# Reading a quad's query and key rows by chunk of tokens, and storing its maxima's rows in two transfers

## The chip, the cores and the metric

The kernel runs on one core of a Trainium2 chip. Five engines work side by side, each from its own list of instructions, in that list's order: TensorE (PE in the profile, its weight loads PEld), VectorE (DVE), ScalarE (ACT), GpSimd (POOL) and SyncE (SP). They wait for each other by semaphores. Transfers between device memory and the core's SBUF are issued here by SP and by ACT; each of the two has a DMA queue of its own, q1 (SP) and q10 (ACT), and 16 DMA engines serve both. The metric is the device time of one execution in microseconds, lower is better.

## The reference, cut to what matters

One transformer block with modulated layer norms: attention over a sliding window of 256 tokens with 32 heads of 20 channels, then an MLP, on 2048 tokens of 640 channels, in float32.

```python
def _A_ref(x, wqkv, wo):
    H = 32; Dh = D // H; W = 256
    qkv = (x @ wqkv).reshape(B, S, 3, H, Dh).transpose(2, 0, 3, 1, 4)
    q, k, v = qkv[0], qkv[1], qkv[2]
    scores = jnp.einsum("bhqd,bhkd->bhqk", q, k) * (Dh ** -0.5)
    mask = (idx[:, None] - idx[None, :] >= 0) & (idx[:, None] - idx[None, :] < W)
    scores = jnp.where(mask[None, None], scores, -1e9)
    p = _softmax(scores, axis=-1)
    o = jnp.einsum("bhqk,bhkd->bhqd", p, v)
    return o.transpose(0, 2, 1, 3).reshape(B, S, D) @ wo
...
h = _layernorm(x) * (1 + ca) + sa
x = x + ga * _A_ref(h, A_wqkv, A_wo)
h = _layernorm(x) * (1 + cb) + sb
x = x + gb * _B_ref(h, B_w1, B_b1, B_w2, B_b2)
```

## The kernel before

**Stages.** Up to some 50 us the kernel computes the modulation, the first layer norm and the first projections. From there (the first score product starts at 49.6 us) to about 690 us runs the attention, with the rest of the projections and then the output projection laid into it, piece by piece. From 690 us on the MLP runs; the change touches nothing of it.

**How the attention is tiled.** The 2048 tokens are two halves (`HALF` = 1024) of eight query blocks of 128 tokens (`NQB`), the 32 heads are eight quads of four (`QUADS`). The main loop (L1263) has one iteration for each half, quad and query block, `t` = 0 to 127, and some more to drain. So a quad takes eight iterations. In iteration `t` the program does two things for two different quads.

- *Scores for the maximum* (`s_batch`, `s_max`): one query block against its three key blocks, on PE into the tile `s`; DVE masks and reduces them to a maximum for each query and head, `nm`. This is quad `t // 8`.
- *Scores for the softmax* (`e_batch`, `e_mask`, `e_exp`), `LAG` = 11 iterations later: the same products, but transposed, into `e`, with the maximum already subtracted; ACT takes the exponential into `pt`, DVE and POOL mask, and PE then multiplies with the values (tile `o`).

The subtraction costs nothing extra on PE. Queries and keys of a quad lie in SBUF as `qbuf` and `kbuf`, two heads' pairs to a tile, each head on 60 partitions (20 channels, three parts each that make up float32 products). Two further partitions of each head, rows 60 and 61, hold the negative maximum as a high and a low part in `qbuf` and ones in `kbuf`. The `s` products read 60 rows, the `e` products 62. So the first `e` matmul of a quad has to wait until the quad's maxima stand in rows 60 and 61 of `qbuf`.

**How the maxima get there.** After the quad's last query block DVE splits `nm` into the two parts (`m_split`, tile `mh`). In the next iteration, `t` a multiple of 8, PE transposes `mh` into the PSUM tile `pm`, and ACT copies it to the SBUF tile `mt` (`m_rows`). Then ACT issues four DMAs from `mt` into rows 60 and 61 (`m_store`): two, for the first pair of heads, at the end of this iteration, and two, for the second pair, at the end of the next one. Each moves 16 rows of 512 B, 8 KB. The quad's first `e` product stands in the third iteration after that multiple of 8.

**How queries and keys get there.** The projections' results are written to device memory (`q_scr`, `k_scr`) by SP, when a unit of 128 channels and 512 tokens (`CHUNK`) is done (`rows_out`), and read back by SP in the layout above (`rows_in`). `rows_in` is called once for the queries and once for the keys of each quad and half, and issues two DMAs, one for each head of a pair: 60 partitions by two pairs by 1024 tokens, 480 KB, and in the second half 1280 tokens of keys, 600 KB. The slots for this, `qb_` and `kb_`, are four deep (`NSLOT`).

**What sets the order.** `plan` maps iteration and quarter to pieces of work. For the reads (L1182) a quad's `due` is its first iteration; its queries are read at `due - READ`, 8 iterations ahead, its keys one iteration later, both in the last quarter, but not before two iterations after the last projection that they need (`over_at`), and not before their slot is free. So a quad's reads usually fall in the first two iterations of the quad before it, the same in which ACT stores that quad's predecessor's maxima.

**DMA semaphores.** The framework gives every DMA, of SP and ACT alike, one of eight semaphores in turn, and a DMA isn't issued before the transfer that had its semaphore last, eight DMAs back, has landed. An engine that waits for this holds everything behind it in its list.

All engine calls go through one helper, so every row of the profile names L112, and instructions are told apart by their tiles.

Of the kernel before, what the change touches and what calls it, by code (L numbers as in the profile page):

```python
# [21 lines left out]
HALF = 1024  # L22
HEADS = (0, 2, 1, 3)
NQB = HALF // P
QUADS = H // 4
CHUNK = 512
VW = 21
VQ = 4 * VW + 11
NSLOT = 4
NVB = 5  # L30
LAG = 11
# [15 lines left out]
    (1, "q00", "k00", "q10", "k10", "q01", "k01", "q11", "k11", "v0", "v1", "q2", "k2", "q3", "k3", "v2", "v3", "q4", "k4", "v4"),  # L47
)
FAST = 10
READ = 8  # L50
LAST = 112

V_COST = 1.7
# [38 lines left out]
def f32(ap):  # L92
    return ap.bitcast(F32)
# [24 lines left out]
def block_kernel(ctx: ExitStack, tc: tile.TileContext, x, wqkv, wo, w1, b1, w2, b2, c, crow, wmod, wcol, sel, outT):  # L118
    core = tc.nc
    nc = Ordered(tc)  # L120
# [256 lines left out]
    qb_ = [att.tile([P, 2, HALF], F32R, name=f"qbuf{i}") for i in range(NSLOT)]  # L377
    kb_ = [att.tile([P, 2, 256 + HALF], F32R, name=f"kbuf{i}") for i in range(NSLOT)]
# [11 lines left out]
    def qbuf(half, pair):  # L390
        return qb_[(half * QUADS + pair // 2) % NSLOT][:, pair % 2]

    def kbuf(half, pair):
        return kb_[(half * QUADS + pair // 2) % NSLOT][:, pair % 2]

    def rows_in(half, quad, kind):

        i = (half * QUADS + quad) % NSLOT
        src = qk_scr[kind].rearrange("(Q a e d) l s -> Q e (d l) a s", a=2, e=2, d=DH)[quad]
        to = qb_[i] if kind == 0 else kb_[i] if half else kb_[i][:, :, 256:]  # L400
        c0 = half * (HALF - 256 * kind)
        for e in range(2):
            nc.sync.dma_start(f32(to[64 * e : 64 * e + 60]), src[e][:, :, c0 : c0 + to.shape[2]])
        if kind:
            there.add((half, quad))

    def vblk(half, quad, kb):
        if half == 1 and kb < 0:
# [1 line left out]
        return vq_[(half * QUADS + quad) % NVB][:, kb]  # L410

    writes, first = [], {}
    there = {(0, 0)}
    quads = {}
    now = [-1]
    done_v = set()
# [103 lines left out]
    def score_banks(kind, name):  # L520
        t = pools[kind].tile([P, 4 * 384], F32, tag=kind, name=name)
        return t, t.rearrange("p (h n) -> p h n", n=384)
# [45 lines left out]
    def s_batch(it):  # L568
        half, quad, qb, g = it["key"]
        if qb == 0:  # L570
            it["quad"]["nm"] = att.tile([P, 4, NQB], F32, tag="nm", bufs=2, name=f"nm{half}_{quad}")
        t, s = score_banks("s", f"s{half}_{quad}_{qb}")
        c0 = 384 - P * min(g + 1, 3)
        parts = []
        for h in HEADS:
            pair, r = 2 * quad + h // 2, slice(64 * (h % 2), 64 * (h % 2) + 60)
            assert (half, quad) in there
            k0 = 256 + (qb - 2) * P + c0
            parts.append([(
                c0, 384 - c0, qbuf(half, pair)[r, qb * P : (qb + 1) * P],  # L580
                lambda off, n, k=kbuf(half, pair), r=r, k0=k0: k[r, k0 + off : k0 + off + n],
            )])
        return (t, parts), s, c0
# [5 lines left out]
        nc.vector.tensor_reduce(it["quad"]["nm"][:, :, it["key"][2]], s[:, :, max(c0, P) : 384], AX.X, ALU.max)  # L589

    mh = att.tile([P, P], F32R, name="mh")
    mh_parts = mh[:, 0:64].rearrange("p (h l q) -> p h l q", h=4, l=2)
    nc.vector.memset(f32(mh)[:, 64:P], 0.0)

    def m_split(it):
        nm, hi, lo = it["quad"]["nm"], mh_parts[:, :, 0], mh_parts[:, :, 1]
        nc.vector.tensor_scalar(hi, nm, -1.0, None, ALU.mult)
        nc.vector.scalar_tensor_tensor(lo, nm, -1.0, f32(hi), ALU.mult, ALU.subtract)

    def m_rows(it):  # L600
        half, quad, _, _ = it["key"]
        ps = aside([P, P], f"pm{half}_{quad}")
        transpose(ps, f32(mh), idn)
        mt = att.tile([64, P], F32, tag="mt", name=f"mt{half}_{quad}")
        nc.scalar.copy(mt, ps[0:64])
        it["mt"] = mt

    def m_store(it, a):
        half, quad, _, _ = it["key"]
        for e in range(2):  # L610
            r = 64 * e + 60
            i = HEADS.index(2 * a + e)
            nc.scalar.dma_start(f32(qbuf(half, 2 * quad + a)[r : r + 2, :]), it["mt"][16 * i : 16 * i + 16])


    def e_parts(it):
# [9 lines left out]
    def e_batch(it):  # L626
        half, quad, i = it["key"]
        t, e = score_banks("e", f"e{half}_{quad}_{i}")
        parts = []
        for h in HEADS:  # L630
            pair, r = 2 * quad + h // 2, slice(64 * (h % 2), 64 * (h % 2) + 62)
            parts.append([(
                col, n, kbuf(half, pair)[r, 256 + kb * P : 256 + (kb + 1) * P],
                lambda off, n, q=qbuf(half, pair), r=r, q0=q0: q[r, q0 * P + off : q0 * P + off + n],
            ) for kb, q0, q1, col, n in e_parts(it)[0]])
        return (t, parts), e

# [460 lines left out]
    def put(t, h, *gos):  # L1098
        plan.setdefault((t, h), []).extend(gos)
# [47 lines left out]
    lo, hi = 4.0, 16.0  # L1147
    for _ in range(30):
        room = (lo + hi) / 2
        lo, hi = (lo, room) if lay_units(room)[0] <= LAST else (room, hi)  # L1150
    _, where, turns = lay_units(hi)
    ready_w = [(seq[0][0], 0)]
    for i, key, c2, pieces, ev in where:
        t0, t1 = pieces[0][0], pieces[-1][0]
# [26 lines left out]
            put(t1, 3, *ev)  # L1181
    for half in range(2):  # L1182
        over_at = {}
        for _, key, _, pieces, _ in where:
            if key[0] == half:
                over_at[key[1:]] = pieces[-1][0]
        for quad in range(QUADS):
            if half or quad:
                js = range(4 * quad * DH // P, (4 * quad * DH + 4 * DH - 1) // P + 1)
                due = 8 * (half * QUADS + quad)  # L1190
                t = due - READ
                for kind in range(2):
                    t = max([t, due - 8 * NSLOT + LAG + 8] + [over_at.get((kind, j), -9) + 2 for j in js])
                    assert t < due - 1, (half, quad, t)
                    put(max(t, 0), 3, lambda half=half, quad=quad, kind=kind: rows_in(half, quad, kind))
                    t += 1
    for n, ((g, at), lo) in enumerate(zip(((2, 0), (4, 1), (3, 2), (5, None)), MODS)):
        steps, rows = mod_steps(g, at)
        spread(plan, [step(1, f) for f in steps], lo[0], lo[1])
        t = int(lo[1])  # L1200
        for f in rows:
            t = take_aside(t, f) + 1
    for ch, when in turns.items():
# [7 lines left out]
        t = when  # L1211
        for kt in range(KT):
            t = take_aside(t, lambda gos=turn[3 * kt : 3 * kt + 3]: [go() for _, go in gos]) + 1
# [34 lines left out]
    s_items, e_items = [], []  # L1248
# [7 lines left out]
    n = len(s_items)  # L1256
# [6 lines left out]
    for t in range(n + LAG + PVLAG + 4):  # L1263
        now[0] = t
        si = s_items[t] if t < n else None
        u = t - LAG
        ei = e_items[u] if 0 <= u < n else None
        if t == n:
            sco_ctx.close()
            pools["t"] = ctx.enter_context(  # L1270
                tc.tile_pool(name="ps_t", bufs=1, space=PSUM, side="left", reuse_waits="tile")
            )
        turn_m = 8 <= t <= n and t % 8 == 0
        batches = []
# [12 lines left out]
        if ei and ei["kbs"]:  # L1287
            e_exp(ei, e)
        if si:
            s_max(si, *got)  # L1290
            if t % NQB == NQB - 1:
                m_split(si)
        rows_out()
        for h in range(4):
            if h == 1 and turn_m:
                m_rows(s_items[t - 1])
            for go in plan.pop((t, h), ()):
                go()
        for a in range(2):
            if 8 <= t - a <= n and (t - a) % 8 == 0:  # L1300
                m_store(s_items[t - a - 1], a)
        for key in pv_at.get(t, ()):
            pv_store(*key)
    assert not writes and not plan
# [19 lines left out]
    for ch in range(nch):  # L1324
        yhi, ylo = ([y[:, kt] for kt in range(KT)] for y in yT[ch % 2])
        ts = slice(ch * CHUNK, (ch + 1) * CHUNK)
        lo, hi = (4, 9) if ch == 0 else (4 * ch + 5, 4 * ch + 9)
# [98 lines left out]
```

## Time and profile before

| | before |
|---|---|
| median of 3 runs | 1093.26 us (1092.42 to 1093.41) |
| the profiled execution's own time | 1094.34 us |
| its span, from the first to the last instruction | 1092.3 us |
| granted TensorE clock, mean over the span | 0.941 |
| attention from the first quad's maxima on, 97.0 to 690.3 us | 593.3 us, PE busy for 505.88 |
| MLP, 690 to 1092.3 us | 402.3 us, PE busy for 397.69 |
| DMA traffic | 91392 packets, 152.88 MB, 140 GB/s over the span |

The profile names a group of instructions by engine, operation and tiles, output first: `e<-qbuf,kbuf` is the softmax score product, `qbuf<-mt` a store of maxima, `qbuf<-q_scr` and `kbuf<-k_scr` reads of rows. ACTq and SPq are those engines' lists of issues. A wait is put down to what ended it. Busy time of PE is modelled, and a busy PE need not be PE at its peak. Over 40 equal slices of the span the granted clock (in tenths) and the share of the 16 DMA engines' time go like this:

```profile
PEclk8899899999899999989976968899999999999999
DMA  8357658726548717871573111424442244213313
```

The DMA engines are busy for much of the attention and little of the MLP, and the clock falls below full in some slices of the attention.

### The profile page before, as it was taken

Reading aid. Unit: us, or ns where it says so; the run is one execution under the profiler, and the core shown is the slowest. Engines: PE = TensorE matmul, PEld = TensorE weight load, DVE = VectorE, ACT = ScalarE, POOL = GpSimd, SP = SyncE. Lnnn points to the kernel's source line nnn. Section 1 sums busy time; section 2 is a strip of 40 time slices with the busy share of each in tenths; the row PEclk is TensorE's granted clock in tenths of the full one; section 3 lists DMA queues with packets and bytes.
Section 4 is the critical chain, followed back from the end, with each engine's and each line's share of the span. In section 5 each row is a group of like instructions: output and inputs, shape, how many; then the busy total and the mean of one; then the engine's idle time right before and its main releaser. Section 6 shows DMA issues by size and latency. Waiting matters only on the chain.

```text
span 1092.3 us, 19853 instructions
## 1 busy us (share of the span) xinstructions
PE 986.5 (90%) x7712; PEld 776.2 (71%) x7712; DVE 579.0 (53%) x943; ACT 444.2 (41%) x773; POOL 510.9 (47%) x702
## 2 busy tenths in 40 slices
PE   7998899699798888889987887999999999999998
PEld 6665666566576666667665665788888888888886
DVE  6643767687476586757656854345443334332212
ACT  3633354365454344435443444443343323333222
POOL 4233445466565244634442654366555545642221
PEclk8899899999899999989976968899999999999999
DMA  8357658726548717871573111424442244213313
GB/s 278 134 188 188 196 163 255 198 85 188 167 143 255 204 58 242 254 203 49 157 182 115 54 41 59 133 89 151 150 126 75 83 130 139 61 49 102 104 49 108
DMA packets 91392, 152.88 MB, mean 140 GB/s; under 512 B 8068, under 2 KB 41476, under 8 KB 91300
## 3 DMA queue, kind: packets, MB, share of 16 engines
q1 hardware_dynamic: 80932, 142.71, 43.7%
q10 hardware_dynamic: 10368, 8.92, 2.7%
q8 instruction: 61, 1.00, 0.4%
q14 instruction: 31, 0.25, 0.1%
HBM read 99.17 MB, written 51.58 MB: 138 GB/s over the span
## 4 chain that ended last, share of the span: by engine, by line
PE 63%; DMA 15%; DVE 8%; POOL 5%; ACT 4%; issue 3%; SPq 1%; ACTq 0%; POOLq 0%; DVEq 0%
PE h L112 15%; PE out L112 15%; PE pp L112 10%; DMA qbuf<-mt 6%; PE wo L112 6%; PE o L112 5%; PE e L112 5%; PE s L112 4%; ACT pt L112 3%; DVE nm L112 2%; DVE e L112 2%; DMA kbuf<-k_scr 2%; DMA wraw<-in_wqkv 1%; DVE s L112 1%; POOL wlo L112 1%
## 5 line engine op out<-in xcount | busy, mean ns | idle before, releaser
L112 POOL TENSOR_SCALAR_AFFINE_SELECT pt<-pt 128x512 f32<-128x512 f32 x192 | 129.1, 673 | 205.7 <-ACT pt L112 185.7
L112 PE MATMUL e<-qbuf,kbuf 62*128 62x128 f32 (+2 forms) x792 | 128.2, 342 | 58.2 <-DMA qbuf<-mt 37.0
L112 PEld LDWEIGHTS e<-qbuf,kbuf 62*128 62x128 f32 x792 | 89.3, 205 | 102.3 <-ACT pt L112 43.2
L112 DVE TENSOR_REDUCE nm<-s 128x4 f32<-128x1024 f32 (+1 forms) x128 | 152.6, 1193 | 4.4
L112 POOL TENSOR_TENSOR w2lo<-w2r,w2hi 128x640 fp32r<-128x640 f32 x48 | 75.6, 1574 | 154.3 <-ACT w2hi L112 154.1
L112 ACT ACTIVATE pt<-e 128x1024 f32<-128x1024 f32 (+1 forms) x120 | 133.8, 1115 | 31.6 <-DVE e L112 30.7
L112 ACT COPY oT<-o 128x128 f32<-128x128 f32 x128 | 34.0, 266 | 251.7 <-PE o L112 228.3
L112 PE MATMUL s<-kbuf,qbuf 60*128 60x256 f32 (+2 forms) x744 | 118.9, 315 | 19.3 <-DVE nm L112 12.1
L112 DVE COPY_PREDICATED e<-mask_t,e 128x512 f32<-128x512 uint32 x96 | 66.6, 694 | 123.2 <-PE s L112 66.8
L112 PE MATMUL pp<-hhi,whi 128*128 128x512 f32 x275 | 122.7, 446 | 3.7 <-ACT hhi L112 1.5
L112 PEld LDWEIGHTS s<-kbuf,qbuf 60*128 60x128 f32 x744 | 99.0, 200 | 36.4 <-issue 10.3
L112 PE MATMUL pp<-hlo,whi 128*128 128x512 f32 x275 | 115.4, 420 | 2.7 <-POOL hlo L112 2.7
L112 PE MATMUL pp<-hhi,wlo 128*128 128x512 f32 x275 | 115.7, 421 | 1.0 <-POOL wlo L112 1.0
L112 DVE CAST ghi<-g 128x512 fp32r<-128x512 f32 x48 | 25.2, 525 | 171.2 <-ACT g L112 171.1
L112 PE MATMUL o<-pt,vbuf 128*32 128x128 f32 x2688 | 111.8, 301 | 0.4 <-ACT oT L112 0.4
L112 POOL TENSOR_TENSOR wlo<-wraw,whi 128x128 fp32r<-128x128 f32 x185 | 81.2, 470 | 39.7 <-ACT whi L112 39.7
L112 PE MATMUL h<-yhi,w1hi 128*128 128x512 f32 x240 | 95.8, 399 | 0.4 <-ACT oT L112 0.4
L112 PE MATMUL out<-ghi,w2hi 128*128 128x512 f32 x240 | 96.2, 401 | 0.0
L112 PE MATMUL h<-ylo,w1hi 128*128 128x512 f32 x240 | 94.0, 392 | 0.0
L112 PE MATMUL h<-yhi,w1lo 128*128 128x512 f32 x240 | 93.9, 391 | 0.0
L112 PE MATMUL out<-ghi,w2lo 128*128 128x512 f32 x240 | 93.9, 391 | 0.0
L112 PE MATMUL out<-glo,w2hi 128*128 128x512 f32 x240 | 93.9, 391 | 0.0
(166 smaller groups left out, 1846.9 us busy)
## 6 DMA issues: line engine op xcount, KB each, us to landing
w2r<-in_w SPq DMA_DIRECT2D x48, 320.0 KB
qbuf<-q_scr SPq DMA_DIRECT2D x30, 480.0 KB
wraw<-in_wqkv SPq DMA_DIRECT2D x38, 320.0 KB
q_scr<-stage SPq DMA_DIRECT2D x20, 512.0 KB
k_scr<-stage SPq DMA_DIRECT2D x20, 512.0 KB
kbuf<-k_scr SPq DMA_DIRECT2D x16, 600.0 KB
o_scr<-oT ACTq DMA_DIRECT2D x64, 128.0 KB
kbuf<-k_scr SPq DMA_DIRECT2D x14, 480.0 KB
```

The source lines that it names most:

```text
L112: return self.tc.keep_in_program_order(op(*args, **kw))
```

## The change

It has three parts.

- `rows_in` takes a chunk `c2` as well and reads 512 tokens of queries or keys (the first chunk of keys in the second half reads 768, with the 256 tokens of the half before). A quad's four DMAs become eight of 240 KB (360 KB for those keys).
- The planner asks for each chunk by its own need: chunk 0 is due with the quad's first iteration, chunk 1 four iterations later; `READ` is 7. A chunk waits only for the projections of its own 512 tokens.
- The rows of `mh` are put in another order (head of the pair, part, pair, block), so that one DMA can fill both pairs of one head's rows. `m_rows` issues the two DMAs, 32 rows of 512 B each, right behind the copy to `mt`; `m_store` and its calls are gone.

```diff
-READ = 8
+READ = 7
...
-    def rows_in(half, quad, kind):
+    def rows_in(half, quad, kind, c2):
...
-        to = qb_[i] if kind == 0 else kb_[i] if half else kb_[i][:, :, 256:]
-        c0 = half * (HALF - 256 * kind)
+        to = (qb_, kb_)[kind][i]
+
+        c0, n = c2 * CHUNK, CHUNK
+        if kind and (c2 or not half):
+            c0 += 256
+        elif kind:
+            n += 256
+        t0 = half * HALF + c0 - 256 * kind
         for e in range(2):
-            nc.sync.dma_start(f32(to[64 * e : 64 * e + 60]), src[e][:, :, c0 : c0 + to.shape[2]])
+            nc.sync.dma_start(f32(to[64 * e : 64 * e + 60, :, c0 : c0 + n]), src[e][:, :, t0 : t0 + n])
...
-    mh_parts = mh[:, 0:64].rearrange("p (h l q) -> p h l q", h=4, l=2)
+    mh_parts = mh[:, 0:64].rearrange("p (e l r) -> p e l r", e=2, l=2)
...
-        nm, hi, lo = it["quad"]["nm"], mh_parts[:, :, 0], mh_parts[:, :, 1]
+        nm, hi, lo = it["quad"]["nm"].rearrange("p (e a) q -> p e (a q)", e=2), mh_parts[:, :, 0], mh_parts[:, :, 1]
...
         nc.scalar.copy(mt, ps[0:64])
-        it["mt"] = mt
-
-    def m_store(it, a):
-        half, quad, _, _ = it["key"]
         for e in range(2):
-            r = 64 * e + 60
-            i = HEADS.index(2 * a + e)
-            nc.scalar.dma_start(f32(qbuf(half, 2 * quad + a)[r : r + 2, :]), it["mt"][16 * i : 16 * i + 16])
+            to = qb_[(half * QUADS + quad) % NSLOT][64 * e + 60 : 64 * e + 62]
+            nc.scalar.dma_start(f32(to), mt[32 * e : 32 * e + 32])
...
-                t = due - READ
-                for kind in range(2):
-                    t = max([t, due - 8 * NSLOT + LAG + 8] + [over_at.get((kind, j), -9) + 2 for j in js])
-                    assert t < due - 1, (half, quad, t)
-                    put(max(t, 0), 3, lambda half=half, quad=quad, kind=kind: rows_in(half, quad, kind))
-                    t += 1
+                for c2 in range(2):
+                    t = due + 4 * c2 - READ
+                    for kind in range(2):
+                        t = max([t, due - 8 * NSLOT + LAG + 8] + [over_at.get((kind, j, c2), -9) + 2 for j in js])
+                        assert t < due + 4 * c2 - 1, (half, quad, c2, t)
+                        put(max(t, 0), 3, lambda half=half, quad=quad, kind=kind, c2=c2: rows_in(half, quad, kind, c2))
+                        t += 1
...
-        for a in range(2):
-            if 8 <= t - a <= n and (t - a) % 8 == 0:
-                m_store(s_items[t - a - 1], a)
```

On ACT, at the fourth quad of the first half (iterations 32 and 33; `oT` and `pt` belong to the quad before it, `stage` and `pf` to a projection, `whi` to its weights), this stood before:

```order
L112 COPY mt_3_2114<-pm_3_2112 64x128
L112 DMA qbuf_96<-mt_3_2114 2x8x128 x2
L112 DMA o_scr<-oT_2_1_2038 128x256
L112 COPY oT_2_2_2166<-o_2_4_2153 128x128
L112 ACTIVATE pt_2_6_2168<-e_2_6_2133 128x1536
L112 CAST whi_2182<-wraw_1952 128x640
L112 ACTIVATE stage_1_4_2190<-pp_1_4_2105 128x512
L112 ACTIVATE pf_1_4_2192<-pp_1_4_2105 128x512
L112 DMA qbuf_96<-mt_3_2114 2x8x128 x2
L112 COPY oT_2_2_2166<-o_2_5_2209 128x128
```

and this stands there now:

```order
L112 COPY mt_3_2124<-pm_3_2122 64x128
L112 DMA qbuf_96<-mt_3_2124 2x16x128 x2
L112 DMA o_scr<-oT_2_1_2048 128x256
L112 COPY oT_2_2_2174<-o_2_4_2161 128x128
L112 ACTIVATE pt_2_6_2176<-e_2_6_2141 128x1536
L112 CAST whi_2190<-wraw_1958 128x640
L112 ACTIVATE stage_1_4_2198<-pp_1_4_2115 128x512
L112 ACTIVATE pf_1_4_2200<-pp_1_4_2115 128x512
L112 COPY oT_2_2_2174<-o_2_5_2215 128x128
```

The second pair's stores are gone from behind `pf`, and the pair behind the copy moves twice the rows. Where a projection's evacuation falls in iteration 32 itself, as at the first quad, the stores also move ahead of its `stage` and `pf`.

On SP, about the same place (`qbuf_94` and `kbuf_98` are the sixth quad's slots, `stage` rows written by a projection, `wraw` weights), before:

```order
L112 DMA wraw_2103<-in_wqkv 128x640
L112 DMA qbuf_94<-q_scr 60x2x1024 x2
L112 DMA kbuf_98<-k_scr 60x2x1024 x2
L112 DMA k_scr<-stage_1_4_2190 128x2x512
L112 DMA k_scr<-stage_1_4_2190 128x512
L112 DMA wraw_2227<-in_wqkv 128x640
L112 DMA wraw_2340<-in_wqkv 128x640
L112 DMA q_scr<-stage_0_4_2458 128x2x512
```

and now:

```order
L112 DMA wraw_2113<-in_wqkv 128x640
L112 DMA qbuf_94<-q_scr 60x2x512 x2
L112 DMA k_scr<-stage_1_4_2198 128x2x512
L112 DMA k_scr<-stage_1_4_2198 128x512
L112 DMA wraw_2233<-in_wqkv 128x640
L112 DMA kbuf_98<-k_scr 60x2x512 x2
L112 DMA wraw_2348<-in_wqkv 128x640
L112 DMA qbuf_94<-q_scr 60x2x512 x2
L112 DMA kbuf_98<-k_scr 60x2x512 x2
L112 DMA q_scr<-stage_0_4_2468 128x2x512
```

Four reads that stood together ahead of a projection's stores are now four pairs with the stores and weights between them. The lists of PE, DVE and POOL keep their order.

More of the change, by code (lines that the diff above doesn't have):

```diff
@@ L394, in kbuf @@
         return kb_[(half * QUADS + pair // 2) % NSLOT][:, pair % 2]
-    def rows_in(half, quad, kind):
+    def rows_in(half, quad, kind, c2):
         i = (half * QUADS + quad) % NSLOT
         src = qk_scr[kind].rearrange("(Q a e d) l s -> Q e (d l) a s", a=2, e=2, d=DH)[quad]
-        to = qb_[i] if kind == 0 else kb_[i] if half else kb_[i][:, :, 256:]
-        c0 = half * (HALF - 256 * kind)
+        to = (qb_, kb_)[kind][i]
[5 more added lines that the diff above has]
+        t0 = half * HALF + c0 - 256 * kind
         for e in range(2):
-            nc.sync.dma_start(f32(to[64 * e : 64 * e + 60]), src[e][:, :, c0 : c0 + to.shape[2]])
-        if kind:
-            there.add((half, quad))
+            nc.sync.dma_start(f32(to[64 * e : 64 * e + 60, :, c0 : c0 + n]), src[e][:, :, t0 : t0 + n])
+        there.add((half, quad, kind, c2))
     def vblk(half, quad, kb):
@@ L412, in block_kernel @@
     writes, first = [], {}
-    there = {(0, 0)}
+    there = {(0, 0, kind, c2) for kind in range(2) for c2 in range(2)}
     quads = {}
@@ L576, in s_batch @@
             pair, r = 2 * quad + h // 2, slice(64 * (h % 2), 64 * (h % 2) + 60)
-            assert (half, quad) in there
+            assert all((half, quad, kind, qb // 4) in there for kind in range(2))
             k0 = 256 + (qb - 2) * P + c0
@@ L1183, in block_kernel @@
         over_at = {}
-        for _, key, _, pieces, _ in where:
+        for _, key, c2, pieces, _ in where:
             if key[0] == half:
-                over_at[key[1:]] = pieces[-1][0]
+                over_at[(*key[1:], c2)] = pieces[-1][0]
         for quad in range(QUADS):
```

## The prediction

> **What bounds the kernel now.** I read the page first, for the engines' shares and the chain that ended last.
>
> ```profile
> span 1092.3 us, 19853 instructions
> ...
> PE 986.5 (90%) x7712; PEld 776.2 (71%) x7712; DVE 579.0 (53%) x943; ACT 444.2 (41%) x773; POOL 510.9 (47%) x702
> ...
> PE h L112 15%; PE out L112 15%; PE pp L112 10%; DMA qbuf<-mt 6%; PE wo L112 6%; PE o L112 5%; PE e L112 5%; PE s L112 4%; ACT pt L112 3%; DVE nm L112 2%; DVE e L112 2%; DMA kbuf<-k_scr 2%; DMA wraw<-in_wqkv 1%; DVE s L112 1%; POOL wlo L112 1%
> ```
>
> PE is busy for 90% of the span, and PE's matmuls lead the chain. Its largest entry that is no arithmetic is the store of the maxima's rows, `qbuf<-mt`, with 6%. So the second view is PE's waits between 60 and 690 us, the attention part (columns: sum in us, times, longest).
>
> ```profile
> PE e L112 <- DMA qbuf<-mt: 37.0, 14, 4.4
> PE e L112 <- ACT pt L112: 20.7, 23, 2.7
> PE s L112 <- DVE nm L112: 12.1, 23, 1.3
> PE s L112 <- DMA kbuf<-k_scr: 6.6, 3, 3.4
> ```
>
> The change touches the first row and the fourth: 37.0 + 6.6 = 43.6 us in which PE stood and a DMA released it. Where they fall is shown by the third view, busy time by stretch. I cut it where `mt` is copied out of PSUM, once per quad, so each row is one quad's period.
>
> ```profile
> core 0: us, PE busy (x) PEld busy (x) DVE busy (x) ACT busy (x) POOL busy (x), PEclk, DMA share, GB/s
> 97.00:135.60 38.60, 31.71 (x226) 22.55 (x224) 22.50 (x28) 15.29 (x28) 17.69 (x27) 0.87 0.65 197
> ...
> 169.00:200.30 31.30, 29.90 (x320) 21.91 (x321) 22.41 (x30) 16.60 (x32) 17.39 (x30) 1.00 0.72 215
> 200.30:239.90 39.60, 31.08 (x326) 22.39 (x326) 27.62 (x43) 18.98 (x34) 22.27 (x36) 0.91 0.49 141
> 239.90:274.80 34.90, 30.91 (x330) 22.35 (x332) 26.52 (x44) 18.68 (x36) 23.16 (x44) 1.00 0.65 181
> 274.80:314.60 39.80, 31.72 (x328) 23.60 (x329) 23.12 (x31) 18.13 (x31) 25.12 (x37) 0.91 0.53 162
> ...
> 349.80:385.80 36.00, 31.68 (x331) 23.24 (x329) 21.19 (x26) 13.95 (x31) 9.36 (x17) 0.95 0.71 188
> 385.80:419.00 33.20, 29.94 (x328) 22.22 (x327) 25.31 (x33) 16.04 (x30) 15.65 (x24) 1.00 0.37 122
> 419.00:454.30 35.30, 31.81 (x364) 23.76 (x362) 27.42 (x37) 16.29 (x28) 18.86 (x26) 1.00 0.78 231
> 454.30:493.90 39.60, 33.33 (x358) 24.83 (x357) 22.77 (x29) 15.66 (x31) 17.64 (x27) 0.91 0.81 221
> 493.90:525.90 32.00, 30.84 (x358) 22.86 (x357) 22.42 (x29) 16.79 (x34) 16.04 (x26) 1.00 0.13 43
> 525.90:566.40 40.50, 33.17 (x354) 24.39 (x352) 24.26 (x30) 17.57 (x32) 17.73 (x23) 0.90 0.65 178
> 566.40:604.80 38.40, 29.81 (x334) 24.10 (x335) 25.39 (x32) 13.21 (x24) 12.78 (x17) 0.67 0.46 126
> ```
>
> The work is nearly the same in each (PE busy for 30 to 33 us), but a period lasts 31.3 to 34.9 us in some and 35.3 to 40.5 in others. One long period in order of time, from the timelines of ACT, SP and PE (start, length, what; the idle time before it in brackets):
>
> ```profile
> 200.06 0.26 ACT L112 COPY mt<-pm 64x128 f32<-64x128 f32 x1 [0.47 <-PE pm L112]
> 200.35 1.28 ACTq L112 DMA_DIRECT2D qbuf<-mt  x2
> ...
> 202.88 1.57 SPq L112 DMA_DIRECT2D qbuf<-q_scr  x2
> ...
> 204.19 0.62 ACTq L112 DMA_DIRECT2D qbuf<-mt  x1
> ...
> 205.28 0.89 SPq L112 DMA_DIRECT2D kbuf<-k_scr  x2
> ...
> 207.55 0.62 ACTq L112 DMA_DIRECT2D qbuf<-mt  x1
> ...
> 212.21 0.38 PE L112 MATMUL e<-qbuf,kbuf 62*128 62x256 f32 x1 [2.85 <-DMA qbuf<-mt]
> 216.41 0.69 PE L112 MATMUL e<-qbuf,kbuf 62*128 62x384 f32 x1 [3.83 <-DMA qbuf<-mt]
> ```
>
> The copy `mt` is done at 200.32. Two of its four stores go out at once, the other two only at 204.19 and 207.55, in the midst of the next quad's row reads. PE has nothing else from 212.21 - 2.85 = 209.36, and loses 2.85 + 3.83 = 6.7 us. The chain shows how long such late stores fly (start, us from issue to landing):
>
> ```profile
> 103.00 8.21 DMA qbuf<-mt
> ...
> 207.55 8.81 DMA qbuf<-mt
> ...
> 280.97 9.51 DMA qbuf<-mt
> ```
>
> That the reads hold them is seen in the DMA queues' packets in two short windows, 135.7 to 141.3 us, just after two stores went out behind a quad's four reads, and 604.8 to 607.2, where two went out with no read about (packets, MB, share of 16 engines; q1 is SP's queue, q10 ACT's):
>
> ```profile
> q1 hardware_dynamic: 425, 1.34, 98.8%
> ...
> q10 hardware_dynamic: 9, 0.01, 0.4%
> ```
>
> ```profile
> q10 hardware_dynamic: 36, 0.02, 2.8%
> ```
>
> In the first, 9 packets of ACT's queue moved in 5.6 us, though two and then three 8 KB stores were out (a store is 16 rows of 512 B). In the second, 36 moved: both stores, within 2.4 us.
>
> **The change part by part.**
>
> *The stores go out earlier.* All of `mt` is now sent right behind the copy. At 620 ns an issue, the second is out by 1.3 us; landing takes 2.4 us more in the quiet case and some 7 in the crowded one. So it lands 2.4 to 8.3 us after the copy, and PE's need came 209.36 - 200.32 = 9.0 us after it. Bounds: all 37.0 us go, or a third of them stays where the queue is full.
>
> *The reads leave the stores' place.* The reads that began in iterations 0 and 1 of a quad's eight now come in iterations 1, 2, 5 and 6, and the stores in 0. The last read starts over one iteration ahead of the store, 4.1 us (the four periods of 31.3 to 34.9 us have a mean of 32.9, in eight iterations); its 480 KB take 2.0 us at the 1.34 MB in 5.6 us of the window above. I take the queue as free in most quads.
>
> *The reads are smaller and some are later.* Bytes stay: a quad's four reads of 480 KB, at 0.24 MB/us, are 8.2 us of a 33 us period. Half-length rows cost between nothing more and, if a packet of 2 KB took as long as one of 4, 8.2 us more of the queue. The nearest row of 2 KB packets, the scratch stores between 345.2 and 347.6 us, is at the first end, so I take nothing:
>
> ```profile
> DMA packets 499, 0.94 MB, mean 390 GB/s; under 512 B 43, under 2 KB 43, under 8 KB 499
> ```
>
> The cover is the time to the need: queries are asked for seven iterations ahead and keys six, 25 to 29 us. One row speaks against this cover, SP's own longest wait; it serves its list in order:
>
> ```profile
> SPq L112 <- POOL stage L112: 174.6, 33, 23.2
> ```
>
> If such a wait falls ahead of a read, the scores wait. But the key reads that the planner put late for want of their producer, three to five iterations ahead, now have a first chunk four to six ahead and a second at six, so I expect the 6.6 us of `PE s <- DMA kbuf<-k_scr` to go.
>
> The Trainium skill speaks against halving: "DMA: Bandwidth & Descriptors", Rules for kernel authors, says to coalesce many small transfers into one, and that under 64 KB one pays mostly overhead. By it the 60 added reads are a loss, and the stores, 8 KB to 16 KB, a gain. The trace doesn't show the loss as a time of the queue: the window with 425 packets is full to 98.8%, so reads follow each other without a hole.
>
> *Issue time.* The split of the maxima on DVE keeps its two instructions of 32 elements. SP has 60 issues more, ACT 32 fewer:
>
> ```profile
> L112 ACTq DMA_DIRECT2D qbuf<-mt x64: 620/621/1240, 97.5 to 648.2; - x64
> L112 SPq DMA_DIRECT2D qbuf<-q_scr x30: 337/386/1634, 71.7 to 562.1; - x30
> L112 ACTq DMA_DIRECT2D o_scr<-oT x64: 321/327/716, 126.7 to 692.1; - x64
> ```
>
> SP: 60 x 0.386 = 23 us over 600, while it mostly waits; nothing. ACT: 32 x 0.62 = 19.8 us less if the larger store costs no more to issue, nothing less if it costs twice (1.24). The store of `oT` has eight times the rows and half the cost, so I take the first. It is ACT time beside a PE that is the bound, with ACT busy for half of each period: nothing in the sum, and if its cover is gone some 1 us a quad.
>
> *What is late next.* Without the stall, PE meets the waits that the short periods have. There, PE idles 31.30 - 29.90 = 1.4, 34.90 - 30.91 = 4.0, 33.20 - 29.94 = 3.3 and 32.00 - 30.84 = 1.2 us, 2.5 on average. In the eight periods of 35.3 us and more it idles 6.9, 8.5, 8.1, 4.3, 3.5, 6.3, 7.3 and 8.6, in all 53.5. If these come down to 2.5 to 3 each, 53.5 - 8 x 2.8 = 31 us go. By PE's waits alone it would be 43.6; by the periods' length (307.8 us for the eight, against 8 x 32.9) 44.6. I take the idle time, the lowest, since waits that end together with another one give back a part: **-31 us**.
>
> The profiled execution took 1094.34 us, 2.0 around its span of 1092.3, and 1.1 more than the median of 1093.26. 1094.3 - 31 = 1063.3 in its terms, 1062 in the median's; I say **1063**.
>
> **The rivals.**
>
> *Half is given back.* PE's next waits, on `pt` (20.7 us) and `nm` (12.1), grow: while PE stood, ACT, DVE and POOL caught up, and POOL is busy for 22 to 25 us of the long periods at 200 and 274. For it: 23 + 23 such waits already. Against it: the short period at 239 has POOL busy for 23.16 us and takes 34.9. It would leave half, -16: 1078 (1071 to 1088).
>
> *Slower: ACT is held by its own issue.* A DMA isn't issued until the transfer that used its semaphore before, eight DMAs back, has landed; the waits tell of this on ACT:
>
> ```profile
> ACT oT L112 <- DMA qbuf<-mt: 6.5, 3, 2.8
> ```
>
> The stores now stand in mid-iteration ahead of a projection's evacuation and the next `pt`. Where the transfer eight back is a row read issued two iterations before and held by SP, ACT stops with all behind it, and PE runs dry. Priced by the wait at 207.55 (204.19 to 207.55 for one issue) at up to 4 us, in all sixteen quads, that is +64 - 31: 1127; in ten, 1103. It decides where that read lands over 5 us after the copy. Against it: the same waits stood ahead of the same `pt` before, at the iteration's end, and the transfers waited for are half as long.
>
> *The stores still wait.* Scratch stores and weights fill the queue as the reads did, the landing stays at 8 to 9 us, and the split reads only stretch over more of it: -4, 1090 (1088 to 1095). Against it: the quiet window's 36 packets.
>
> *More goes than the waits.* The granted clock is 0.87 to 0.91 in five of the eight periods and 1.00 in all four short ones here. If PE's work there is stretched by it, up to 0.13 x 38.6 + 0.09 x (39.6 + 39.8 + 39.6) + 0.10 x 40.5 = 20 us come on top: 1043. Against it: PE's busy time is just 1 to 2 us longer there. "TensorE: Matmul & The Clock Gate" of the Trainium skill (Why this matters for your kernels) asks for no PE-idle gaps over some 3 us, or the clock falls to half; the rows agree with it in sign.
>
> **How the numbers follow.** Forecast (1050 to 1070) 0.60; half given back 0.20; stores still wait 0.06; ACT held 0.09; clock on top 0.05. The range 1050 to 1087 takes in the first two. A change within 0.2%, about what a measurement of this kernel can tell, is 1091.1 to 1095.4: 0.06. Faster 0.85, slower 0.09.
>
> **What would show it.** PE's wait `e <- DMA qbuf<-mt` under 6 us in all and `s <- DMA kbuf<-k_scr` near nothing; the long periods at 33 to 36 us and the short ones as they were; the clock at 0.95 or more up to 566 us; the chain without `qbuf<-mt`. I am wrong if ACT's waits on DMAs grow past 20 us, if PE's waits on `pt` or `s <- DMA` take the room, or if the stores still land 8 us after the copy.

## The result, and the profile after

| | before | after |
|---|---|---|
| median | 1092.84 us (4 runs, 1088.07 to 1093.41) | 1043.09 us (4 runs, 1040.07 to 1045.16) |
| the profiled execution's own time | 1094.34 us | 1042.79 us |
| its span | 1092.3 us | 1040.4 us |
| granted clock, mean | 0.941 | 0.962 |

The ratio is 0.9552, 95% interval [0.9516, 0.9588]: about 50 us faster. The forecast was 1063 with a range of 1050 to 1087. The sign was right and the size was not: 31 us were forecast, and the time lies 7 us below the range.

The page of the changed kernel: span, engines, the granted clock in slices, the chain by engine and by line.

```profile
span 1040.4 us, 19908 instructions
...
PE 972.3 (93%) x7712; PEld 766.4 (74%) x7712; DVE 576.1 (55%) x943; ACT 443.7 (43%) x773; POOL 513.0 (49%) x702
...
PEclk8999999999899999999968978999999999999999
...
PE 75%; DVE 10%; ACT 5%; DMA 3%; POOL 3%; issue 2%; SPq 1%; ACTq 0%; POOLq 0%; DVEq 0%
PE h L112 16%; PE out L112 16%; PE pp L112 14%; PE wo L112 7%; PE o L112 6%; PE e L112 6%; PE s L112 5%; DVE e L112 3%; DVE nm L112 3%; ACT pt L112 3%; DVE s L112 2%; PE ppo L112 2%; DMA kbuf<-k_scr 1%; PE yt L112 1%; PE psx L112 1%
```

The store `qbuf<-mt`, 6% of the chain before, is no entry any more. But PE's own busy time also fell, from 986.5 to 972.3 us with the same 7712 products: a part which the prediction's sum left out. PE's waits between 60 and 690 us begin like this now:

```profile
PE e L112 <- ACT pt L112: 27.7, 28, 2.8
PE s L112 <- DVE nm L112: 9.7, 20, 1.3
```

Both DMA rows, 37.0 and 6.6 us before, are gone. The two that remain were 20.7 and 12.1, so together they grew by 4.6 us: little was given back.

Where the span went is read by cutting both runs at the first copy of `mt` and 402.6 us before the end. The columns are those of the prediction's periods (stretch, length, PE busy, PEld, DVE, ACT, POOL, PEclk, DMA share, GB/s). Before:

```profile
96.80:689.70 592.90, 505.48 (x5350) 376.01 (x5352) 384.61 (x531) 268.03 (x489) 296.28 (x454) 0.91 0.54 156
0.00:96.80 96.80, 82.99 (x413) 64.98 (x414) 52.97 (x138) 40.79 (x70) 33.55 (x57) 0.91 0.61 197
```

After:

```profile
94.40:637.80 543.40, 490.88 (x5360) 364.91 (x5363) 384.66 (x531) 267.95 (x491) 297.33 (x454) 0.94 0.57 172
0.00:94.40 94.40, 83.40 (x413) 66.03 (x414) 50.06 (x138) 40.70 (x69) 34.00 (x57) 0.93 0.57 191
```

The attention is 49.5 us shorter. Length less PE's busy time is its idle time: 592.90 - 505.48 = 87.4 before, 543.40 - 490.88 = 52.5 after, so **34.9 us are idle time and 14.6 us are busy time**. Each figure is from one execution. That PE's products got faster does not hang on that choice: the mean granted clock is 0.961 to 0.967 in the four runs of the changed kernel, and 0.932 to 0.949 in the twelve runs of the kernel before that stood beside the first experiments. But those twelve runs took 1088.03 to 1101.7 us, the longest at the lowest clock, so 14.6 us is a size good to a few us only.

The first 95 us bring 2.4 more. The last 402.6 us hold the same work in both, with PE busy for 398.0 of them.

The same eight quads whose periods were long before, cut at the copies of `mt` again:

```profile
94.70:127.10 32.40, 29.64 (x226) 21.32 (x224) 22.52 (x29) 15.00 (x27) 17.50 (x27) 0.95 0.82 258
...
190.30:223.20 32.90, 31.03 (x326) 21.97 (x324) 27.46 (x43) 19.09 (x34) 22.41 (x36) 0.95 0.55 169
...
257.00:293.40 36.40, 32.48 (x328) 23.79 (x329) 23.91 (x31) 18.20 (x31) 25.32 (x37) 0.91 0.53 165
...
324.00:354.70 30.70, 29.63 (x330) 22.02 (x328) 21.53 (x27) 13.86 (x30) 10.08 (x18) 1.00 0.69 191
...
387.90:421.20 33.30, 31.91 (x364) 23.74 (x362) 27.76 (x37) 16.29 (x28) 18.86 (x26) 1.00 0.82 264
421.20:453.80 32.60, 31.04 (x359) 22.83 (x357) 22.73 (x29) 15.70 (x31) 17.68 (x27) 1.00 0.87 254
...
485.80:517.50 31.70, 29.68 (x354) 22.12 (x352) 23.86 (x30) 17.66 (x31) 17.75 (x23) 1.00 0.67 195
517.50:553.50 36.00, 27.88 (x333) 22.34 (x335) 24.64 (x33) 13.10 (x24) 13.32 (x17) 0.76 0.61 164
```

Their sum is 266.0 us, against 307.8. PE idles 22.7 us in them (266.0 - 243.3), against 53.5, and is busy for 243.3 against 254.3. The idle time falls by 30.8 us, which is the forecast term to within a microsecond; the busy time falls by 11.0, which the forecast had at nothing. The clock in these rows rises from 0.67 to 1.00 before, to 0.76 to 1.00 after, and to 1.00 in four of the eight.

That the same products run faster is seen in the groups of PE's products over the attention (busy us, mean ns | idle before). Before, and after:

```profile
L112 PE MATMUL e<-qbuf,kbuf 62*128 62x128 f32 (+2 forms) x792 | 128.2, 342 | 58.2 <-DMA qbuf<-mt 37.0 <-ACT pt L112 20.7
L112 PE MATMUL s<-kbuf,qbuf 60*128 60x128 f32 (+2 forms) x695 | 111.9, 315 | 19.1 <-DVE nm L112 12.1 <-DMA kbuf<-k_scr 6.6
```

```profile
L112 PE MATMUL e<-qbuf,kbuf 62*128 62x128 f32 (+2 forms) x792 | 121.5, 332 | 28.4 <-ACT pt L112 27.7 <-DMA wraw<-in_wqkv 0.2
...
L112 PE MATMUL s<-kbuf,qbuf 60*128 60x128 f32 (+2 forms) x695 | 105.8, 306 | 10.9 <-DVE nm L112 9.7 <-PE e L112 0.3
```

The same 792 and 695 products take 6.7 and 6.1 us less.

### The profile page after: what moved, and what is told of

It reads as the page before. It is cut to its first block, busy times and chain, and to the rows that moved or that the text cites. A ratio compares the mean times of both kernels' runs of the same rounds, so it can differ in the third digit from the quotient of the medians.

```text
span 1040.4 us, 19908 instructions
## 1 busy us (share of the span) xinstructions
PE 972.3 (93%) x7712; PEld 766.4 (74%) x7712; DVE 576.1 (55%) x943; ACT 443.7 (43%) x773; POOL 513.0 (49%) x702
## 4 chain that ended last, share of the span: by engine, by line
PE 75%; DVE 10%; ACT 5%; DMA 3%; POOL 3%; issue 2%; SPq 1%; ACTq 0%; POOLq 0%; DVEq 0%
PE h L112 16%; PE out L112 16%; PE pp L112 14%; PE wo L112 7%; PE o L112 6%; PE e L112 6%; PE s L112 5%; DVE e L112 3%; DVE nm L112 3%; ACT pt L112 3%; DVE s L112 2%; PE ppo L112 2%; DMA kbuf<-k_scr 1%; PE yt L112 1%; PE psx L112 1%
## 5 line engine op out<-in xcount | busy, mean ns | idle before, releaser
L112 PE MATMUL e<-qbuf,kbuf 62*128 62x128 f32 (+2 forms) x792 | 121.5, 332 | 28.4 <-ACT pt L112 27.7
L112 PEld LDWEIGHTS e<-qbuf,kbuf 62*128 62x128 f32 x792 | 83.8, 195 | 70.5 <-ACT pt L112 48.8
L112 PE MATMUL s<-kbuf,qbuf 60*128 60x256 f32 (+2 forms) x744 | 112.8, 307 | 11.1 <-DVE nm L112 9.7
L112 PEld LDWEIGHTS s<-kbuf,qbuf 60*128 60x128 f32 x744 | 93.6, 193 | 29.1 <-PE e L112 8.2
L112 PE MATMUL o<-pt,vbuf 128*32 128x128 f32 x2688 | 106.7, 291 | 1.4 <-DVE ylo L112 1.1
```

Source lines behind the costliest of these rows:

```text
L112: return self.tc.keep_in_program_order(op(*args, **kw))
```

## The experiments

Two questions were open: which part of the change carries the gain, and whether the 15 us of busy time are a cost of the stalls (the clock after a gap in PE's work) or something else.

### The stores alone

Before, with the two larger stores right behind the copy; the reads stay whole, `READ` 8.

```diff
         nc.scalar.copy(mt, ps[0:64])
-        it["mt"] = mt
+            nc.scalar.dma_start(f32(to), mt[32 * e : 32 * e + 32])
...
-                m_store(s_items[t - a - 1], a)
```

> Only the stores' part of the change: two 16 KB stores right behind the copy; the reads stay whole (480 KB, 8 and 7 iterations ahead). Theory A (the place of the issue decides: a store sent behind the copy lands within 8 us even behind whole reads, and PE needs it at 9): PE's waits on qbuf<-mt fall from 37 to under 8 us, the waits on kbuf<-k_scr stay near 6.6, time 1048 to 1056. Theory B (the reads in the queue decide, early or late): waits on qbuf<-mt stay over 15 us, time 1065 to 1080.

Measured: 1060.53 us, ratio 0.9696 [0.9638, 0.9754], so 34 us faster. PE's waits on DMAs from 60 to 690 us, and the packets of the two queues in one stretch from 327.6 to 333.2 us, right behind two such stores:

```profile
PE e L112 <- DMA qbuf<-mt: 6.8, 5, 2.4
PE s L112 <- DMA kbuf<-k_scr: 5.7, 3, 2.2
```

```profile
q1 hardware_dynamic: 315, 1.26, 94.6%
q10 hardware_dynamic: 10, 0.01, 0.5%
```

The waits are where theory A has them; the time is some 5 us above its range. But a store behind whole reads does not land within 8 us, as theory A had it: in this window 10 packets of ACT's queue moved in 5.6 us, and the chain has the store issued at 327.01 us flying for 11.06 us. And `s` still waits for its keys as before.

### The reads alone

Before, with `rows_in` and the planner of after (chunks, `READ` 7) and the four stores of 8 KB at their old places.

```diff
-READ = 8
+READ = 7
...
-    def rows_in(half, quad, kind):
+    def rows_in(half, quad, kind, c2):
```

> Only the reads' part: chunks, READ 7; the four 8 KB stores where they were, two at the end of the iteration of the copy and two at the end of the next. Theory B: waits on qbuf<-mt under 10 us, time 1045 to 1058. Theory A: the second pair is sent some 7 us after the copy and lands at 9.6 at the earliest, so most quads still wait 1 to 4 us: 15 to 30 us of waits on qbuf<-mt, none on kbuf<-k_scr, time 1062 to 1080.

Measured: 1061.41 us, ratio 0.9699 [0.9648, 0.975], so 33 us faster. Time and wait both lie just below theory A's ranges (1062 to 1080 us, 15 to 30 us) and just above theory B's (1045 to 1058, under 10), so neither is borne out as it was put.

```profile
PE e L112 <- DMA qbuf<-mt: 13.6, 10, 2.7
...
PE e L112 <- DMA kbuf<-k_scr: 1.2, 1, 1.2
```

The stores cost 13.6 us where they stand late but mostly find a free queue, and the wait of `s` for keys is gone. Each half of the change alone brings 33 to 34 us, both together 50. So the parts overlap by some 17 us: in many quads either of them is enough to end the stall.

### Four small stores, early, with whole reads

The first experiment with the maxima's rows in their old order, and so four stores of 8 KB right behind the copy instead of two of 16.

```diff
         nc.scalar.copy(mt, ps[0:64])
+        for a in range(2):
+            m_store(it, a)
...
-                m_store(s_items[t - a - 1], a)
```

> The stores behind the copy, but still four of 8 KB; the reads whole as before. If merging four into two matters by ACT's issue time or by the queue (4 x 0.62 = 2.5 us until the last is out, against 1.3), this is 5 us or more slower than the run with two early stores; if only the place matters, within 4 us of it.

Measured: 1078.62 us, ratio 0.9869 [0.9821, 0.9918]: 18 us slower than with two stores. ACT's longest waits on DMAs, and ACT's timeline at the fourth quad:

```profile
ACT oT L112 <- DMA qbuf<-mt: 27.5, 8, 5.3
ACT whi L112 <- DMA wraw<-in_wqkv: 8.2, 3, 6.2
ACT stage L112 <- DMA qbuf<-mt: 6.4, 2, 3.4
```

```profile
205.76 0.26 ACT L112 COPY mt<-pm 64x128 f32<-64x128 f32 x1 [0.46 <-PE pm L112]
206.06 4.03 ACTq L112 DMA_DIRECT2D qbuf<-mt  x4
210.88 0.33 ACTq L112 DMA_DIRECT2D o_scr<-oT  x1
211.30 0.27 ACT L112 COPY oT<-o 128x128 f32<-128x128 f32 x1 [5.28 <-DMA qbuf<-mt]
```

PE waits for `qbuf<-mt` only 3.3 us here, so the stores are early enough. Yet ACT stands 5.28 us ahead of its next copy: four issues take 4.03 us, and the store of `oT` behind them only goes out at 210.88, after a further hold. This is the rival "ACT is held by its own issue": it is real, with four stores. But most of it is not the hold that the prediction priced. The rows of ACT's waits contain the time in which ACT issues, and where nothing holds them, four issues take 2.6 us. Over the sixteen quads the four take 48.0 us here, of which 16 x 2.6 = 41.6 is plain issuing; the two of the first experiment take 21.6. From the end of the copy to ACT's next instruction it is 55.5 us here against 32.6 there: 23 us more, where the run is 18 us slower. (In this profiled run 4.4 of the span's 15.9 us more than in the first experiment fall before the first copy of `mt`, where the code is the same but for the order of the maxima's rows: 100.9 against 96.5.)

### Four small stores, early, with the reads in chunks

The changed kernel, with the edit of the experiment above.

> The changed kernel with four 8 KB stores behind the copy in place of two of 16 KB. If four early stores cost 18 us beside whole reads because ACT stands at its own issue for the semaphores of transfers eight back: with half-size reads ACT's waits put down to DMAs fall from 48 us to some 20 and the time is 1048 to 1058. If the four issues of 0.62 us themselves cost it, 1056 to 1063. If nothing of it is left: 1043 to 1047.

Measured: 1065.8 us, ratio 0.9761 [0.9733, 0.9789]: 23 us slower than the changed kernel.

```profile
ACT oT L112 <- DMA qbuf<-mt: 35.3, 9, 6.3
...
ACT oT L112 <- DMA qbuf<-q_scr: 6.7, 1, 6.7
```

The attention of its profiled run:

```profile
95.60:663.80 568.20, 503.94 (x5354) 373.78 (x5352) 383.83 (x531) 266.05 (x489) 296.38 (x454) 0.91 0.55 164
```

The time lies above all three ranges that were expected. The expectation that ACT's waits would fall once the reads are smaller was wrong: ACT's waits on DMAs between 60 and 690 us add up to 57.2 us in the experiment above and 68.9 here. In the changed kernel the first of these rows is 5.2 us (shown below). The four issues take 53.5 us over the sixteen quads, again for the most part plain issuing (41.6), against 22.9 for the two of the changed kernel; so of the two reasons that were set against each other the issues themselves are the larger and the hold is the smaller, though the run is slower than was expected of either. PE idles 11.7 us more in the attention than in the changed kernel and is busy for 13.1 more. Early is also no better than late with four stores and chunks: the run with the reads alone took 1061.41 us. So merging four stores into two is worth some 20 us by itself, with either kind of reads, and it is what keeps the early place from costing what it saves.

### The two large stores, late

The changed kernel, with both stores moved to the end of the next iteration.

```diff
+        if 9 <= t <= n + 1 and t % 8 == 1:
+            m_store(s_items[t - 2])
```

> The changed kernel, but its two 16 KB stores at the end of the iteration after the copy, some 7 us later (where the second pair stood before). If the place of the stores still matters once the reads are in chunks: PE's waits on qbuf<-mt come back with 1 to 4 us a quad, 15 to 35 us, and the time is 1060 to 1078. If the chunked reads had made room for a store at any time: waits under 8 us, 1043 to 1050.

Measured: 1061.61 us, ratio 0.9736 [0.9697, 0.9776]: 19 us slower than the changed kernel.

```profile
PE e L112 <- DMA qbuf<-mt: 18.9, 7, 5.9
```

The attention of its profiled run:

```profile
95.30:655.90 560.60, 492.66 (x5360) 365.77 (x5363) 384.44 (x531) 268.15 (x491) 297.26 (x454) 0.94 0.56 167
```

The waits come back, as expected, and the time with them. PE idles 15.4 us more in the attention than in the changed kernel, but is busy for only 1.8 more. Place, number of stores and reads each matter; none of them makes the others needless.

### Whole reads, one iteration later

The first experiment with `READ` 7.

```diff
-READ = 8
+READ = 7
```

> Early stores in two transfers with whole 480 KB reads as in the run with the stores' part alone, but the reads one iteration later (READ 7). If it is the shift away from the stores' iteration that the reads' part brings: waits on qbuf<-mt under 3 us, those on kbuf<-k_scr still 5 to 7, time 1047 to 1054. If the chunks are needed: as the run with the stores alone, 1056 to 1063.

Measured: 1054.92 us, ratio 0.9659 [0.9637, 0.9681].

```profile
PE s L112 <- DMA kbuf<-k_scr: 5.3, 2, 3.1
```

```profile
98.40:650.10 551.70, 494.69 (x5354) 366.92 (x5353) 384.59 (x531) 268.19 (x489) 295.99 (x454) 0.93 0.58 169
```

The waits are as the first case had them; the time lies between the two ranges that were expected. PE hardly waits for the maxima (0.4 us in all), so moving the whole reads out of the stores' way is enough for that. By the medians it brings 6 of the 17 us between the first experiment and the changed kernel, but against their own runs of the kernel before, the intervals of this run and of the first experiment overlap, so these 6 are not clear of noise. The other 12 stand between this run and the changed kernel, and their intervals are apart. In the profiled runs 8.3 of them lie in the attention (551.7 against 543.4): 4.5 us of idle time, about what `s` waits for its keys, and 3.8 us of busy time. The remaining 4.0 lie before the first copy of `mt`, 98.4 against 94.4; over all the runs that stretch lies between 94.4 and 100.9 us, so I don't put them down to the chunks. What the chunks bring is then some 8 us; the run doesn't part what the halving brings from what the later, separate need of the second chunk does.

### The chunks one iteration earlier

The changed kernel with `READ` 8.

> The changed kernel with READ 8: each chunk's reads one iteration earlier, so the queries' reads start again in the iteration of the stores, but behind them. Stores first, reads after: nothing is lost, waits on qbuf<-mt under 3 us, 1040 to 1047. If reads in that iteration hold the stores wherever they stand in it: waits of 5 us and more, 1050 to 1060.

Measured: 1047.16 us, ratio 0.9582 [0.9555, 0.961], against the changed kernel's 0.9552 [0.9516, 0.9588]. The time is 0.2 us past the upper end of the first range that was expected. The intervals overlap; with chunks no difference between the two iterations is shown, and neither kernel waits for the maxima or the keys on PE.

### Gaps filled, waits kept

The kernel before, with 129 products of identity by identity ahead of the first `e` product of nine quads, 4 to 24 each, where PE stood. They go into the tile of `e` before its own products overwrite it, so nothing reads them; the stores and reads, and what they wait for, stay as they were.

```diff
+FILL = {0: 20, 1: 4, 3: 24, 5: 24, 7: 11, 9: 8, 10: 17, 12: 9, 13: 12}
...
+        if ei and ei["kbs"] and ei["key"][2] == 0:
+            for _ in range(FILL.get(8 * ei["key"][0] + ei["key"][1], 0)):
+                matmul(e_tile[:, 0:P], idn, idn, start=True, stop=True)
```

> The kernel before with nothing moved, but with unused 128x128 products (4 to 24 of them, some 1 to 5 us) on PE ahead of the first e product in the nine quads where PE waited for the stores; the waits themselves stay, PE is only kept busy during them. Theory C (the waits cost twice, once as idle time and once as a lower granted clock afterwards, some 11 us of PE's busy time): granted clock in the periods up to 566 us at 0.95 or more, time 1080 to 1088. If the clock costs nothing (busy PE is paced by something else): 1090 to 1097 in spite of the clock.

Measured: 1085.57 us in the median of 9 runs, ratio 0.9917 [0.9879, 0.9956]: 9 us **faster**, with more work. The mean granted clock of the nine runs is 0.958 to 0.969, that of the twelve runs beside them 0.932 to 0.949. The attention of its profiled run (1081.19 us, 4 under that median), the two groups of products shown above and that of the added ones (two records each; a line added ahead of the helper makes its rows L113):

```profile
96.70:676.50 579.80, 518.76 (x5612) 392.68 (x5610) 384.56 (x531) 268.26 (x489) 297.40 (x454) 0.95 0.55 159
```

```profile
L113 PE MATMUL e<-qbuf,kbuf 62*128 62x128 f32 (+2 forms) x792 | 122.5, 327 | 28.7 <-ACT pt L113 23.5 <-DMA qbuf<-mt 4.7
L113 PE MATMUL s<-kbuf,qbuf 60*128 60x128 f32 (+2 forms) x695 | 106.7, 305 | 16.2 <-DVE nm L113 12.4 <-DMA kbuf<-k_scr 3.4
...
L113 PE MATMUL e<-idn 128*128 128x128 f32 x258 | 32.7, 287 | 5.3 <-ACT pt L113 5.3
```

The clock over the attention is 0.95 against 0.91, higher than in the changed kernel (0.94). The kernel's own `e` and `s` products, the same in number and still fed by late stores, take 5.7 and 5.2 us less, nearly as much less as in the changed kernel. So slower products are a cost of the gaps, separate from the waits themselves, and filling the gaps takes it away. PE's wait rows shrink (`qbuf<-mt` to 4.7 us) only because PE is busy while it waits: the idle time of this attention, 61.0 us, and the 32.7 of the added products make 93.7, against 87.4 of idle time before. The kernel's own products are busy for 19.4 us less in this profiled run, so the 9 us are what is left of a larger gain.

The rule of the Trainium skill that the prediction weighed, "TensorE: Matmul & The Clock Gate" (Why this matters for your kernels: no gaps of PE over some 3 us), is borne out here in sign, and the runs give it a price: 9 us net for the gaps of nine quads.

## Why the prediction was right or wrong

**What bounds the kernel.** Right. The long periods were the place, and the late landing of `qbuf<-mt` was the cause: the wait fell from 37.0 us to nothing, and the stores alone (6.8 us left) or the reads alone (13.6) take most of it away.

**What is late next.** The step that failed, in its size: "I take the idle time, the lowest". As a statement on the idle time of the eight periods it held: -31 forecast, -30.8 measured, and 22.7 us over eight periods are 2.84 each, where 2.8 was taken. That they agree so closely is partly luck, for one by one the eight idle from 1.1 to 8.1 us. As the whole sum it was too small by 19 us (21 between the two profiled executions), for two things that it priced at nothing:

- PE's busy time in the same eight periods: -11.0 us, the clock. The prediction saw the cooler rows and set this aside because "PE's busy time is just 1 to 2 us longer there". That is 1 to 2 us times eight; by its own rows it is a mean of 31.8 in the eight periods against 30.4 in the four short ones, times eight 11 us. It had the term in its hand as an argument against the term. The gap-filling run shows it as a cost of its own, 9 us net.
- The rest of the span: the attention outside those eight periods gives 49.5 - 41.8 = 7.7 us, of which 4.1 are idle time and 3.6 busy time, and the start gives 2.4. The largest piece is one period that the prediction left out as not long, before and after:

```profile
314.60:349.80 35.20, 31.02 (x319) 22.63 (x318) 21.26 (x26) 16.35 (x29) 21.57 (x38) 0.95 0.74 221
```

```profile
293.40:324.00 30.60, 29.11 (x320) 21.33 (x318) 20.93 (x26) 16.13 (x29) 20.91 (x37) 1.00 0.76 242
```

This period is 4.6 us shorter: 2.7 of the 6.6 us of waits for keys fell there, and 1.9 us are busy time. The other 3.9 us of waits for keys fell in the long period from 525.9 us, and so were in the sum already.

The estimate from the periods' lengths, 44.6 us, which the prediction worked out and didn't take, was nearest: a length contains the slower clock as well as the wait. For the eight periods themselves 41.8 was measured.

**The stores go out earlier.** Right. PE no longer waits for them. ACT's timeline in the changed kernel:

```profile
190.07 0.26 ACT L112 COPY mt<-pm 64x128 f32<-64x128 f32 x1 [0.47 <-PE pm L112]
190.36 1.30 ACTq L112 DMA_DIRECT2D qbuf<-mt  x2
191.71 0.66 ACTq L112 DMA_DIRECT2D o_scr<-oT  x1
192.63 0.27 ACT L112 COPY oT<-o 128x128 f32<-128x128 f32 x1 [2.30 <-DMA qbuf<-mt]
```

Both are issued within 1.3 us, as forecast, where four took 4.03 us at this quad. The flight of some 7 us that the prediction took for a crowded queue was too short beside whole reads (11.06 us in the first experiment).

**The reads leave the stores' place, and are smaller.** Right, and the doubt about halved transfers was not needed. The prediction read the Trainium skill's rule to coalesce ("DMA: Bandwidth & Descriptors", Rules for kernel authors) as for the stores and against the chunks. For the stores the runs agree, with some 20 us for four turned into two. For the reads no loss shows, and the rule's figure of 64 KB lies below their 240 KB: read by chunk, each as it is needed and with the same bytes, they are 8 to 12 us faster than whole ones at the same `READ`.

**Issue time.** Right in its figures. A store of twice the rows costs the same to issue, and SP's list has room for 30 more issues of queries:

```profile
L112 SPq DMA_DIRECT2D qbuf<-q_scr x60: 315/417/1518, 66.5 to 528.8; - x60
```

```profile
L112 ACTq DMA_DIRECT2D qbuf<-mt x32: 620/622/1239, 94.7 to 592.9; - x32
```

But "nothing in the sum" hid what the merge is for: ACT's time beside a busy PE is free on average, and not right behind `mt`, where the next `oT` and `pt` are waited for; there the two further issues cost 18 and 23 us.

**The rivals.** *Half is given back*: no; the waits on `pt` and `nm` grew by 4.6 us in all. In one period it came true: from 517.5 us PE waits 7.9 us for `pt`, where before, from 566.4, it waited 4.7 for `pt` and 3.6 for the maxima. *ACT is held*: in both runs with four stores, by 27.5 and 35.3 us in the row of `oT` and `qbuf<-mt` alone, most of it issuing. In the changed kernel that row was 6.5 before and is now:

```profile
ACT oT L112 <- DMA qbuf<-mt: 5.2, 2, 2.9
```

At one quad the hold did happen there: behind the two issues at 257.05 us ACT stands for 5.3 us, put down to a row read, and PE behind it for 2.9, in the period with the lowest clock ahead of 517.5 us:

```profile
ACT oT L112 <- DMA kbuf<-k_scr: 5.3, 1, 5.3
```

The sign that the prediction set for it, ACT's waits on DMAs past 20 us, was a bad one: the rows add up to 22.8 us before and 23.6 after. *The stores still wait*: no. *More goes than the waits*: this one came true, and its 1043 is the measured time, though partly by chance: it put 20 us on the clock, without the period at 0.67, where the busy time of the attention fell by 14.6, and the rest is idle time outside the eight periods and the start. It had a chance of 0.05.

**The signs.** The waits and the chain came as said, and the four short periods are at most 1.1 us shorter than they were. The long periods came to 30.7 to 36.4 us instead of 33 to 36, and the clock is 0.91 in one of them ahead of 566 us, from 257.0, where 0.95 was asked, and 0.76 in another, from 517.5.

**What stays open.** Why the time up to the first copy of `mt` differs between the profiled runs, by up to 6.5 us. The chunks change the reads there, but four kernels with the same reads lie between 96.5 and 100.9 us; the longest stretch has a granted clock of 0.86, the shortest 0.93, and what sets that clock no run here shows. And the stretches from 517.5 and 592.2 us still run at a clock of 0.76 and 0.74, with waits for `pt`; products to fill those gaps were not tried. Why the busy time grew so differently beside added idle time, 1.8 us beside 15.4 with two late stores and 13.1 beside 11.7 with four early ones (one execution each), is open too.

## What to carry to other kernels

Where an engine's stall is priced, compare stretches with and without it by their length, not by the waits: the length also holds what the stall does to the work behind it, here a slower clock for about a third as much again in eight periods (11.0 us beside 30.8), though not in every run. When a small, urgent transfer shares the DMA engines with large ones, three things count together: when it is issued, how many issues it takes, and what is in the queue by then; moving it early in four pieces gave half of its gain back through the issuing engine. And a wait that the prediction expects to go has to be in its sum, also where it stands outside the stretches that were counted.

## What was not expected of the hardware

- Extra products sped the kernel up: 129 of them, 32.7 us of PE's records, made it 9 us faster, ratio 0.9917 [0.9879, 0.9956].
- Transfers of a few rows hardly advanced while large reads of the other queue ran: 10 packets of q10 against 315 of q1 in 5.6 us, just after two stores of 32 rows were issued.
- Issuing a store into two partitions took ACT 620 ns with 16 rows and 622 with 32, while the 128-row store of `oT` took 327. Four such issues in a row held ACT for 2.6 us where nothing else did.
